# Attention output products by column halves, and the layout of three PSUM banks

## The chip, the cores and the metric

The kernel runs on one core of one Trainium2 chip. The metric is the time of one execution on the device in microseconds (us). Runs are compared by their medians; the profile is of one execution.

## The reference

One transformer block with adaptive layer norm: sliding-window attention over a key/value cache, then a gated feed-forward part. x is 2048 x 576, 32 query heads share 16 key/value heads of width 128, the window is the last 512 keys, and the feed-forward width is 4608.

```python
mod = (_silu(c) @ w_mod).reshape(c.shape[0], 6, 1, -1)
sa, ca, ga, sb, cb, gb = (mod[:, 0], mod[:, 1], mod[:, 2], mod[:, 3], mod[:, 4], mod[:, 5])
h = _layernorm(x, axis=-1) * (1 + ca) + sa
x = x + ga * _A_ref(h, A_k_cache, A_v_cache, A_wq, A_wo)
h = _layernorm(x, axis=-1) * (1 + cb) + sb
x = x + gb * _B_ref(h, B_w1, B_w3, B_w2)
...
# _A_ref: q = x @ wq by heads; softmax(q k^T * Dh**-0.5) v; heads side by side @ wo
# _B_ref: (silu(x @ w1) * (x @ w3)) @ w2
```

## The kernel before

The 2048 rows are four blocks of 512 (b), each of four row tiles of 128 (t). Every product is done in float16 pieces, a high and a low part, so one product is three matmuls: high x high, high x low, low x high.

**Slots and steps.** A slot is one query head on one row block: 128 slots, two heads of a group one after the other, and such two slots are a pair. The main loop runs over slots i and, in each, over four steps t = 0 to 3. The instructions of every engine stand in the order in which this loop writes them; nothing is reordered later. In step t of slot i TensorE (PE) gets: at t = 1 the transposes of one tile of the slot before (`turn`, into a PSUM tile named `pt`); three matmuls for the scores of row tile t (`pss`); at t = 0 to 2 a third of the next slot's query projection (`pq`); one piece of an older pair's output product; then the step's tasks. At the slot's end come twelve matmuls of the value product (`values`, `po`).

**The output product.** `attend_out` multiplies the two normalized heads `o` of a pair (slots 2*pair and 2*pair + 1) with `wo` (128 x 576 for each head) and adds the result to `acc`. A row tile takes two steps, one head in each (j = 0, then j = 1): `back` goes through the three float16 combinations and, in each, through the two column halves of 288. The halves lie in the two PSUM banks of the tile `E` (its name in the trace is `pe`). After j = 1, VectorE (DVE) adds both halves to `acc` with one SCALAR_TENSOR_TENSOR (L617), called the add below. The products of a pair start at step t = 2 of slot 2*pair + 4, so j = 0 falls on even t and j = 1 on odd t. Some steps also put a small matmul for a scale factor into a corner of E (`sum_peaks`, `in_total`, `out_total`), which DVE copies out right after the add.

**PSUM.** Eight banks: two tiles `A` (`pq`, `po`, `py`), two tiles `S` (`pss`, `px`), the two-bank tile E, and two one-bank tiles `T` (`pt`). The T tiles serve `turn` and also the transposes of normalized rows, five per row block (m = 0 to 4; `turn_rows`, L257), from which ScalarE (ACT), and in the kernel's first microseconds DVE too, makes h: `modulate` (L272 later, L266 to L270 at the start), `modulate_first` (L284 and L286, for the very first block) and `store_h` (L656). For blocks 2 and 3, and again for blocks 0 and 1 before the feed-forward part, these five stand in the steps t = 0, 1, 2 of one slot and t = 0, 1 of the next, after the step's output product. When attention ends, the T tiles make room for a second two-bank tile for the feed-forward part (`turning.close()`).

**Waits.** The tile layer that records the program puts semaphore waits before an instruction, for every tile that it reads or writes: what another engine still does with that tile has to be done first.

Of the kernel before, what the change touches and what calls it, by code (L numbers as in the profile page):

```python
# [20 lines left out]
P = 128  # L21
# [27 lines left out]
def tile_block(  # L49
# [110 lines left out]
    def mod_cols(wm, name, one, tag):  # L160

        ps = t_bank() if tag == "T" else bank(tag, f"ps_{name}")
# [12 lines left out]
    def mod_rows(wm, kind):  # L175

        vec = gate_rows[kind]
        wm = wm[0]
        for h in range(2):
            for d in (0, 3):  # L180
                nc.tensor.matmul(
                    E[:, h, :HALF], ones, wm[:, d, h * HALF : (h + 1) * HALF], start=d == 0, stop=d == 3
                )
        nc.vector.tensor_copy(half_split(vec), E[:, :, :HALF])
        return vec
# [67 lines left out]
    def turn_rows(b, m, tag):  # L253

        ps = t_bank() if tag == "T" else bank(tag, "ps_n")
        for t in range(ST):
            nc.tensor.transpose(ps[:, t * P : (t + 1) * P], norms[b][1][t][:, m * P : (m + 1) * P], ident)  # L257
        return ps
# [69 lines left out]
    def sum_peaks(g, lo, hi, ps=None):  # L328

        ps = E[:, 1, 400:416] if ps is None else ps  # L330
        nc.tensor.matmul(ps[:, lo:hi], peak_ones, tops[g][:, lo:hi], start=True, stop=True)

    def take_sums(g, lo, hi, ps=None):

        ps = E[:, 1, 400:416] if ps is None else ps
        nc.vector.tensor_copy(peaks[g][:, 5 + lo : 5 + hi], ps[:, lo:hi])
# [116 lines left out]
    def back(ps, o, w, t, first, last):  # L453

        rows = slice(t * P, (t + 1) * P)
        for n, (x, y) in enumerate(((0, 0), (0, 1), (1, 0))):
            for h in range(2):
                nc.tensor.matmul(  # L458
                    ps[:, h, :HALF],
                    o[:, x, rows],  # L460
                    w[:, y, h * HALF : (h + 1) * HALF],
                    start=first and n == 0,
                    stop=last and n == 2,
                )
# [144 lines left out]
    def attend_out(pair, t, j, total):  # L609
        u, _, b = slots[2 * pair]  # L610
        lane[0] += j == 0
        ps = spare()
        back(ps, state[2 * pair + j]["o"], wos[u][:, j], t, j == 0, j == 1)
        if j == 1:
            run(*total)
            a = half_split(acc[b][:, t, :])
            nc.vector.scalar_tensor_tensor(  # L617
                a, ps[:, :, :HALF], factors[:, uses[u][0], 2:3], a, op0=ALU.mult, op1=ALU.add
            )
# [3 lines left out]
    for pair in range(n // 2):  # L623
        for k in range(2 * ST):
# [6 lines left out]
            outs.setdefault(when, []).append((pair, *divmod(k, 2)))  # L631
# [17 lines left out]
    def store_h(b, m, tag, tag_out):  # L649
# [9 lines left out]
        store_later(hd[b][m * P : m * P + n, :], hf[:n], ("s", b, m) if tag == "T" else None)  # L659
# [485 lines left out]
    lane = [0, ()]  # L1145

# [12 lines left out]
    def in_total(f):  # L1159

        m = peak_cols[:, 4 * (f % 2) :][:, :4]
        for part in range(2):
            peak = m[:, 2 * part + 1 : 2 * part + 2]
            nc.tensor.matmul(
                spare()[:, 1, 408:410], peak.to_broadcast([P, P]), m[:, 2 * part : 2 * part + 2],
# [3 lines left out]
    def in_taken(f):  # L1169
        nc.vector.tensor_copy(stats[:, f, :], spare()[:, 1, 408:410])  # L1170
# [24 lines left out]
    def out_total(p):  # L1195
        nc.tensor.matmul(spare()[:, 1, 410:411], peak_ones, peak_cols[:, 8 + p % 2 : 9 + p % 2], start=True, stop=True)

    def out_taken(p):
        nc.vector.tensor_copy(out_down[:, p : p + 1], spare()[:, 1, 410:411])
# [236 lines left out]
    def make_h(b, m, early=False):  # L1436
        modulate(hT[b], m, turn_rows(b, m, "T"), vecs["shift", "a"], vecs["gain", "a"], early)
# [34 lines left out]
    for b, i in ((0, 111), (1, 114)):  # L1472
        norm(i, b)
        for m in range(DC + 1):
            at(i + 1 + m // 3, m % 3, store_h, b, m, "T", "raw")
# [50 lines left out]
    at(106, 2, make_cols, "shift", "b", 3, 0.0, "T")  # L1526
    at(109, 2, make_cols, "gain", "b", 4, 1.0, "T")
    at(109, 3, lambda: spread_peaks("b", mlp_small))
    at(110, 1, lambda: scale_cols("b", t_bank(), mlp_small, 2.0**-8))
# [24 lines left out]
    turned = [turn_rows(0, m, "TTAAS"[m]) for m in range(DC + 1)]  # L1554
# [44 lines left out]
    for i in range(n + 2):  # L1599
        run(i, -1)  # L1600
        for t in range(ST):
# [121 lines left out]
```

## Time and profile before

| | us |
|---|---|
| median of 3 runs | 2752.52 |
| lowest, highest | 2752.24, 2756.41 |
| the profiled execution's own time | 2752.42 |
| its span | 2750.3 |
| PE busy in it | 2682.3 (98%) |
| DVE busy | 1995.2 (73%) |
| POOL (GpSimd) busy | 1873.1 (68%) |
| ACT busy | 1622.9 (59%) |

In a row of the timeline stand the start in us from the span's start, how long the row's instructions took together, the engine, the line, the operation, out<-in, the shapes, the count, and in brackets the engine's idle time before it and what ended that. A matmul's end is modelled and overlaps the next one's start, so an idle time in brackets is smaller than the pause from start to start.

### The profile page before, as it was taken

Reading aid. Unit: us, or ns where it says so; the run is one execution under the profiler, and the core shown is the slowest. Engines: PE = TensorE matmul, PEld = TensorE weight load, DVE = VectorE, ACT = ScalarE, POOL = GpSimd, SP = SyncE. Lnnn points to the kernel's source line nnn. Section 1 sums busy time; section 2 is a strip of 40 time slices with the busy share of each in tenths; the row PEclk is TensorE's granted clock in tenths of the full one; section 3 lists DMA queues with packets and bytes.
Section 4 is the critical chain, followed back from the end, with each engine's and each line's share of the span. In section 5 each row is a group of like instructions: output and inputs, shape, how many; then the busy total and the mean of one; then the engine's idle time right before and its main releaser. Section 6 shows DMA issues by size and latency. Waiting matters only on the chain.

```text
span 2750.3 us, 44762 instructions
## 1 busy us (share of the span) xinstructions
PE 2682.3 (98%) x15406; PEld 1511.8 (55%) x15406; DVE 1995.2 (73%) x3550; ACT 1622.9 (59%) x3026; POOL 1873.1 (68%) x1745
## 2 busy tenths in 40 slices
PE   6899999999999999999999999999999999999998
PEld 3455555555555555555555555555555555555555
DVE  7877787878787787887876667777776666566566
ACT  6776778777777778777677635544443323333332
POOL 4677888888888877777669637688774465334435
PEclk9999999999999999999999999999999999999999
DMA  6778888778787888978879945656643434333332
GB/s 196 174 171 198 195 180 192 168 182 188 171 187 165 190 193 193 214 178 208 194 182 219 241 134 171 200 165 201 208 160 107 157 122 129 102 103 111 105 109 85
DMA packets 593460, 463.84 MB, mean 169 GB/s; under 512 B 442704, under 2 KB 472528, under 8 KB 592208
## 3 DMA queue, kind: packets, MB, share of 16 engines
q1 hardware_dynamic: 592944, 460.69, 65.4%
q8 instruction: 121, 1.98, 0.3%
q14 instruction: 107, 0.88, 0.1%
q10 hardware_dynamic: 288, 0.30, 0.0%
HBM read 264.19 MB, written 95.99 MB: 131 GB/s over the span
## 4 chain that ended last, share of the span: by engine, by line
PE 50%; DVE 2%; POOL 2%; issue 1%; DMA 1%; ACT 1%; SPq 0%; POOLq 0%; DVEq 0%; ACTq 0%
PE py L874 15%; PE px L874 11%; PE pf L959 6%; PE pe L959 6%; PE pe L458 3%; PE po L587 3%; PE pss L508 2%; PE pq L435 2%; DMA r<-row 1%; PE pt L548 0%; POOL acc L913 0%; PE pq L439 0%; DMA row<-l 0%; DVE table L512 0%; POOL sums L913 0%
## 5 line engine op out<-in xcount | busy, mean ns | idle before, releaser
L562 POOL TENSOR_TENSOR hp<-p,hp 128x512 f16<-128x512 f32 x384 | 448.8, 1171 | 269.6 <-ACT hp L557 154.1
L525 ACT ACTIVATE p<-pss,table,factors 128x512 f32<-128x512 f32 x512 | 396.8, 775 | 355.1 <-DVE table L513 175.7
L874 PEld LDWEIGHTS <-wset 128*128 128x128 f16 x3528 | 344.2, 98 | 337.4 <-issue 4.0
L512 DVE TENSOR_REDUCE table<-pss 128x1 f32<-128x512 f32 x512 | 350.3, 684 | 199.4 <-PE pss L508 198.8
L874 PE MATMUL py<-hset,wset 128*128 128x512 f16 x2016 | 482.1, 379 | 0.0
L458 PE MATMUL pe<-o 128*128 128x288 f16 x3024 | 453.4, 286 | 11.6 <-DVE acc L617 10.7
L508 PE MATMUL pss<-k,qT 128*128 128x512 f16 x1536 | 418.0, 380 | 13.2 <-ACT p L525 10.6
L458 PEld LDWEIGHTS <-o 128*128 128x128 f16 x3072 | 300.8, 98 | 186.1 <-issue 17.5
L587 PE MATMUL po<-ptw,v 128*128 128x512 f16 x1536 | 358.6, 381 | 7.8 <-DVE ptw L577 2.7
L874 PE MATMUL px<-hset,wset 128*128 128x512 f16 x1512 | 361.5, 379 | 2.1 <-ACT p L525 2.1
L94 POOL TENSOR_TENSOR akv<-u,akv 128x512 f16<-128x512 f32 x141 | 164.8, 1178 | 178.4 <-ACT akv L93 170.5
L435 PE MATMUL pq<-hT,wq 128*128 128x512 f16 x1092 | 280.6, 379 | 0.0
L557 ACT CAST hp<-p 128x512 f16<-128x512 f32 x384 | 237.3, 618 | 14.1 <-DMA ptw<-hp 0.9
L587 PEld LDWEIGHTS <-v 128*128 128x128 f16 x1536 | 147.8, 98 | 175.0 <-issue 16.2
L959 PEld LDWEIGHTS <-akv 128*128 128x128 f16 x1728 | 169.1, 98 | 89.3 <-issue 0.8
L508 PEld LDWEIGHTS <-qT 128*128 128x128 f16 x1536 | 147.6, 98 | 127.2 <-issue 14.8
L617 DVE SCALAR_TENSOR_TENSOR acc<-pe,factors,acc 128x576 f32<-128x576 f32 x252 | 204.3, 811 | 4.8 <-PE pe L458 4.8
L607 POOL TENSOR_TENSOR o<-on,o 128x512 f16<-128x512 f32 x128 | 150.2, 1174 | 54.0 <-ACT o L606 52.0
L435 PEld LDWEIGHTS <-wq 128*128 128x128 f16 x1092 | 106.9, 98 | 127.4 <-issue 1.0
L953 DVE SCALAR_TENSOR_TENSOR acc<-pf,table,acc 128x576 f32<-128x576 f32 x140 | 113.5, 811 | 79.3 <-PE pf L959 79.3
L1052 ACT COPY u<-py 128x512 f32<-128x512 f32 x72 | 42.2, 586 | 201.3 <-PE py L874 199.4
L1045 ACT ACTIVATE s<-s,table 128x512 f32<-128x512 f32 x72 | 52.0, 722 | 175.1 <-DVE s L1044 175.0
(254 smaller groups left out, 4789.0 us busy)
## 6 DMA issues: line engine op xcount, KB each, us to landing
wset<-wd SPq DMA_DIRECT2D x213, 320.0 KB, 3.2
r<-row SPq DMA_DIRECT2D x128, 256.0 KB, 3.9
oset<-od SPq DMA_DIRECT2D x106, 288.0 KB, 3.2
wraw<-in_w SPq DMA_DIRECT2D x36, 768.0 KB, 5.5
wd<-wmade SPq DMA_DIRECT2D x75, 320.0 KB, 3.2
wset<-wd SPq DMA_DIRECT2D x71, 160.0 KB, 2.2
w2raw<-in_w SPq DMA_DIRECT2D x19, 576.0 KB, 5.2
wd<-ring SPq DMA_DIRECT2D x33, 320.0 KB, 2.8
```

The lines of the kernel that those rows point to most:

```text
L94: eng.tensor_sub(halves[:, 1], src, halves[:, 0])
L435: nc.tensor.matmul(ps, w[:, k // 2, m, :], hT[:, DC + m if k == 1 else m, :], start=s == 0, stop=False)
L458: nc.tensor.matmul(ps[:, h, :HALF], o[:, x, rows], w[:, y, h * HALF : (h + 1) * HALF], start=first and n == 0, stop=last and n == 2,)
L508: nc.tensor.matmul(pss, q[:, x, rows], k[:, y, :], start=n == 0, stop=n == 2)
L512: nc.vector.tensor_reduce(nm[:, 0:1], pss, axis=AX.X, op=ALU.max, negate=True)
L525: nc.scalar.activation(p, pss, AF.Exp, bias=nm[:, 1:2], scale=factor, accum_out=st["l"][:, t : t + 1])
L557: nc.scalar.copy(hp[:, 0, :], state[i]["p", t])
L562: nc.gpsimd.tensor_sub(hp[:, 1, :], state[i].pop(("p", t)), hp[:, 0, :])
L587: nc.tensor.matmul(po, v[:, x, c, :], pt[:, y, c, :], start=c == 0 and n == 0, stop=c == KC - 1 and n == 2)
L617: nc.vector.scalar_tensor_tensor(a, ps[:, :, :HALF], factors[:, uses[u][0], 2:3], a, op0=ALU.mult, op1=ALU.add)
L874: nc.tensor.matmul(ps, w[:, a, :], h[:, b, :], start=start and n == 0, stop=stop and n == 6, skip_group_check=True)
L959: nc.tensor.matmul(ps[:, h, :HALF], a[:, rows], w[:, b, :], start=m == 0, stop=m == 2)
```

## The change

E becomes a tile of three banks, in the pool that T was in, and T has one buffer instead of two. The output product of a row tile is now cut by column halves: the first step does the right half (h = 1) for both heads, the second the left half (h = 0) for both. The left half lies in bank 0, the right half in bank 1 or 2, in turn from tile to tile (`lane[0]`). The add reads both halves through one strided view, banks 0 and 1 or banks 0 and 2. The transposes of normalized rows, the column sums of the modulation (`mod_cols`) and `scale_cols` now write the bank of E that is not in use for a right half (`idle()`); the very first ones and those of the second block go to banks 1 and 2 by name. The small sums go to bank 0.

```diff
-    E = psum.tile([P, 2, 512], F32, tag="E", name="pe", bufs=1)
     turning = ExitStack()
-    tpool = turning.enter_context(tc.tile_pool(name="tpool", bufs=2, space=PSUM))
-
-    def t_bank():
-        return tpool.tile([P, 512], F32, tag="T", name="pt")
+    tpool = turning.enter_context(tc.tile_pool(name="tpool", bufs=1, space=PSUM))
+    E = tpool.tile([P, 3, 512], F32, tag="E", name="pe")
+    lane = [1, ()]
+
+    def both_halves():
+        return lane[1][lane[0] % 2][:, :, :HALF] if lane[1] else E[:, 0 : lane[0] + 1 : lane[0], :HALF]
+
+    def idle():
+        return E[:, 3 - lane[0], :]
...
     def turn_rows(b, m, tag):
-        ps = t_bank() if tag == "T" else bank(tag, "ps_n")
+        ps = idle() if tag == "E" else E[:, int(tag), :] if tag in "012" else bank(tag, "ps_n")
...
-    def back(ps, o, w, t, first, last):
+    def back(ps, o, w, t, h, first, last):
         rows = slice(t * P, (t + 1) * P)
         for n, (x, y) in enumerate(((0, 0), (0, 1), (1, 0))):
-            for h in range(2):
-                nc.tensor.matmul(
-                    ps[:, h, :HALF],
...
+            nc.tensor.matmul(
+                ps,
...
-        ps = st["t"] = t_bank().rearrange("p (j n) -> p j n", j=KC)
+        ps = st["t"] = tpool.tile([P, KC, P], F32, tag="T", name="pt")
...
-    def attend_out(pair, t, j, total):
+    def attend_out(pair, t, h, total):
         u, _, b = slots[2 * pair]
-        lane[0] += j == 0
-        ps = spare()
-        back(ps, state[2 * pair + j]["o"], wos[u][:, j], t, j == 0, j == 1)
-        if j == 1:
+        if h:
+            lane[0] = 3 - lane[0]
+        for j in range(2):
+            back(both_halves()[:, h], state[2 * pair + j]["o"], wos[u][:, j], t, h, j == 0, j == 1)
+        if not h:
             run(*total)
             a = half_split(acc[b][:, t, :])
             nc.vector.scalar_tensor_tensor(
-                a, ps[:, :, :HALF], factors[:, uses[u][0], 2:3], a, op0=ALU.mult, op1=ALU.add
+                a, both_halves(), factors[:, uses[u][0], 2:3], a, op0=ALU.mult, op1=ALU.add
             )
...
-            outs.setdefault(when, []).append((pair, *divmod(k, 2)))
+            outs.setdefault(when, []).append((pair, k // 2, 1 - k % 2))
...
     def make_h(b, m, early=False):
-        modulate(hT[b], m, turn_rows(b, m, "T"), vecs["shift", "a"], vecs["gain", "a"], early)
+        modulate(hT[b], m, turn_rows(b, m, str(1 + m % 2) if early else "E"), vecs["shift", "a"], vecs["gain", "a"], early)
...
-    at(110, 1, lambda: scale_cols("b", t_bank(), mlp_small, 2.0**-8))
+    at(110, 1, lambda: scale_cols("b", idle(), mlp_small, 2.0**-8))
...
-    turned = [turn_rows(0, m, "TTAAS"[m]) for m in range(DC + 1)]
+    turned = [turn_rows(0, m, "12AAS"[m]) for m in range(DC + 1)]
...
-                    lane[1] = (E, after.tile([P, 2, 512], F32, tag="T2", name="pf"))
+                    lane[1] = tuple(after.tile([P, 2, 512], F32, tag=tag, name=tag) for tag in ("pe", "pf"))
```

Four places in the order of PE's instructions, each before and then after the change. In brackets stand the semaphores that a row waits for. L257 became L262, L458 became L462, L508 became L512, L435 and L445 became L440 and L450.

The start of a row tile's output product, in a plain slot: the end of a third of a query (`pq`), then the first matmuls of the product (`pe<-o`).

```order
L435 MATMUL pq<-hT,wq 128x512
L458 LDWEIGHTS o
L458 MATMUL pe<-o 128x288 [waits DVE_49]
L458 LDWEIGHTS o
L458 MATMUL pe<-o 128x288
```

```order
L440 MATMUL pq<-hT,wq 128x512
L462 LDWEIGHTS o
L462 MATMUL pe<-o 128x288 [waits DVE_49]
L462 LDWEIGHTS o
L462 MATMUL pe<-o 128x288
```

The matmul is now the first of a right half, in a bank that the tile before did not use. It keeps a wait for DVE, and the count that it waits for is, before and after, that of the add of the tile before (or, where a small sum was copied out behind that add, of the copy).

Step t = 1 of the first of the slots with transposes of normalized rows: the end of the output product, the four transposes (`<-ident,xn`), the next scores.

```order
L458 MATMUL pe<-o 128x288
L257 MATMUL pt<-ident,xn 128x128 [waits Activation_49]
L257 MATMUL pt<-ident,xn 128x128 x3
L508 LDWEIGHTS qT
L508 MATMUL pss<-k,qT 128x512
```

```order
L462 MATMUL pe<-o 128x288
L262 MATMUL pe<-ident,xn 128x128 [waits DVE_49]
L262 MATMUL pe<-ident,xn 128x128 x3
L512 LDWEIGHTS qT
L512 MATMUL pss<-k,qT 128x512
```

The wait for an older read of a T tile became a wait for DVE; its count is that of the add whose products stand right ahead of it.

Step t = 2 of the same slot and the start of t = 3: the transposes, the scores, and the second piece of the output product.

```order
L257 MATMUL pt<-ident,xn 128x128 [waits Activation_49]
L257 MATMUL pt<-ident,xn 128x128 x3
L508 LDWEIGHTS qT
L508 MATMUL pss<-k,qT 128x512
L508 LDWEIGHTS qT
L508 MATMUL pss<-k,qT 128x512
L508 LDWEIGHTS qT
L508 MATMUL pss<-k,qT 128x512
L458 LDWEIGHTS o
L458 MATMUL pe<-o 128x288
L458 LDWEIGHTS o
```

```order
L262 MATMUL pe<-ident,xn 128x128 x4
L512 LDWEIGHTS qT
L512 MATMUL pss<-k,qT 128x512
L512 LDWEIGHTS qT
L512 MATMUL pss<-k,qT 128x512
L512 LDWEIGHTS qT
L512 MATMUL pss<-k,qT 128x512
L462 LDWEIGHTS o
L462 MATMUL pe<-o 128x288 [waits Activation_49]
L462 LDWEIGHTS o
```

The second piece, now a left half in bank 0, got a wait for ACT; its count is that of ACT's read (`modulate`) of the transposes four rows up.

The start of the kernel: a warming matmul, then the first query (`pe<-hT,wq`).

```order
L223 MATMUL ps_warm<-ident,ones 128x128 x2
L445 LDWEIGHTS wq [waits Activation_49]
L445 MATMUL pe<-hT,wq 128x512 [waits Activation_49]
L445 LDWEIGHTS wq
L445 MATMUL pe<-hT,wq 128x512 [waits DVE_49]
L445 LDWEIGHTS wq
L445 MATMUL pe<-hT,wq 128x512 [waits Activation_49]
```

```order
L228 MATMUL ps_warm<-ident,ones 128x128 x2
L450 LDWEIGHTS wq [waits Activation_49]
L450 MATMUL pe<-hT,wq 128x512 [waits Activation_49]
L450 LDWEIGHTS wq
L450 MATMUL pe<-hT,wq 128x512
L450 LDWEIGHTS wq
L450 MATMUL pe<-hT,wq 128x512
```

Before, each matmul waits for the piece of h that it reads. Now the first waits for ACT's fifth read in `modulate_first`, the last one that touches a bank of E, and the next ones need no wait of their own.

More of the change, by code (lines that the diff above doesn't have):

```diff
@@ L160, in mod_cols @@
     def mod_cols(wm, name, one, tag):
-        ps = t_bank() if tag == "T" else bank(tag, f"ps_{name}")
+        ps = idle() if tag == "E" else bank(tag, f"ps_{name}")
         wm = wm[0]
@@ L181, in mod_rows @@
                 nc.tensor.matmul(
-                    E[:, h, :HALF], ones, wm[:, d, h * HALF : (h + 1) * HALF], start=d == 0, stop=d == 3
+                    ps[:, h], ones, wm[:, d, h * HALF : (h + 1) * HALF], start=d == 0, stop=d == 3
                 )
-        nc.vector.tensor_copy(half_split(vec), E[:, :, :HALF])
+        nc.vector.tensor_copy(half_split(vec), ps)
         return vec
@@ L451, in project_first @@
                     nc.tensor.matmul(ps, w[:, k, DC, :], hT[:, 2 * DC, :], start=False, stop=False)
-    def back(ps, o, w, t, first, last):
+    def back(ps, o, w, t, h, first, last):
         rows = slice(t * P, (t + 1) * P)
         for n, (x, y) in enumerate(((0, 0), (0, 1), (1, 0))):
-            for h in range(2):
-                nc.tensor.matmul(
-                    ps[:, h, :HALF],
[L460 to L464, printed above, removed]
+            nc.tensor.matmul(
+                ps,
+                o[:, x, rows],
+                w[:, y, h * HALF : (h + 1) * HALF],
+                start=first and n == 0,
+                stop=last and n == 2,
+            )
     QP = (range(0, 5), range(5, 10), range(10, 14))
@@ L1164, in in_total @@
             nc.tensor.matmul(
-                spare()[:, 1, 408:410], peak.to_broadcast([P, P]), m[:, 2 * part : 2 * part + 2],
+                spare()[:, 0, 408:410], peak.to_broadcast([P, P]), m[:, 2 * part : 2 * part + 2],
                 start=part == 0, stop=part == 1,
@@ L1195, in out_total @@
     def out_total(p):
-        nc.tensor.matmul(spare()[:, 1, 410:411], peak_ones, peak_cols[:, 8 + p % 2 : 9 + p % 2], start=True, stop=True)
+        nc.tensor.matmul(spare()[:, 0, 410:411], peak_ones, peak_cols[:, 8 + p % 2 : 9 + p % 2], start=True, stop=True)
     def out_taken(p):
-        nc.vector.tensor_copy(out_down[:, p : p + 1], spare()[:, 1, 410:411])
+        nc.vector.tensor_copy(out_down[:, p : p + 1], spare()[:, 0, 410:411])
     def out_scale(p):
```

16 lines of the change are left out of this document (8 added, 8 removed).

## The prediction

> **What bounds the kernel now.** I read the page's busy shares first, then PE's waits, then the rows of the places that the change touches.
>
> ```profile
> PE 2682.3 (98%) x15406; PEld 1511.8 (55%) x15406; DVE 1995.2 (73%) x3550; ACT 1622.9 (59%) x3026; POOL 1873.1 (68%) x1745
> L458 PE MATMUL pe<-o 128*128 128x288 f16 x3024 | 453.4, 286 | 11.6 <-DVE acc L617 10.7
> PE pe L458 <- DVE acc L617: 10.7, 11, 2.0
> PE pss L508 <- ACT p L525: 10.6, 14, 2.6
> ```
>
> PE is the bound; any time that it gains or loses is the kernel's, unless a later wait takes it back. All that the output product can give back is its wait for the add of the tile before: 10.7 us in 11 places. That is the ceiling of what a free third bank could give.
>
> **The change part by part.**
>
> *The wait for the add stays: 0.* The right half goes to an unused bank, but in the built program its first matmul still waits for the add of the tile before, for nearly all tiles, exactly as the first matmul did. Waits are made for the tile E as a whole, not for its banks. So I take nothing off. Bounds: 0 and -10.7.
>
> *Six matmuls a step, in one bank: 0.* The feed-forward product does three in one bank one after the other:
>
> ```profile
> 2003.24 0.90 PE L959 MATMUL pf<-oset,aah 128*128 128x288 f16 x6
> ```
>
> Six take 0.90 there, as in the attention rows below, where the banks alternate.
>
> *Five transposes per row block now write E.* The first block's rows, PE, then DVE, then ACT:
>
> ```profile
> 141.76 0.90 PE L458 MATMUL pe<-o 128*128 128x288 f16 x6
> 142.49 0.60 PE L257 MATMUL pt<-ident,xn 128*128 128x128 f32 x4
> 142.93 0.81 PE L508 MATMUL pss<-k,qT 128*128 128x512 f16 x3
> 146.26 0.90 PE L458 MATMUL pe<-o 128*128 128x288 f16 x6
> ...
> 142.74 0.82 DVE L617 SCALAR_TENSOR_TENSOR acc<-pe,factors,acc 128x576 f32<-128x576 f32 x1
> 144.45 0.64 DVE L512 TENSOR_REDUCE table<-pss 128x1 f32<-128x512 f32 x1
> ...
> 145.37 0.78 ACT L525 ACTIVATE p<-pss,table,factors 128x512 f32<-128x512 f32 x1 [0.57 <-DVE table L513]
> 147.28 0.77 ACT L272 ACTIVATE hf<-pt,mod_a 128x512 f32<-128x512 f32 x1
> ```
>
> (a) At t = 1 the transposes now wait for the add just issued. They started at 142.49; the add ends at 142.74 + 0.82 = 143.56, so PE stands 1.07. This happens twice per block (m = 1 and m = 4) in four blocks: eight times. The last of the eight:
>
> ```profile
> 1441.99 0.60 PE L257 MATMUL pt<-ident,xn 128*128 128x128 f32 x4
> 1442.24 0.81 DVE L617 SCALAR_TENSOR_TENSOR acc<-pe,factors,acc 128x576 f32<-128x576 f32 x1
> ```
>
> 1442.24 + 0.81 - 1441.99 = 1.06. Eight times 1.07 is 8.6 us. Queued behind the waiting transposes are the next scores, so DVE's maximum and ACT's exponential start later too.
>
> (b) At t = 3 the left half waits for ACT's read of the transposes made at t = 2. In the first block the read ended at 147.28 + 0.77 = 148.05 and the product started at 146.26: 1.79 late. The other three blocks:
>
> ```profile
> 183.61 0.90 PE L458 MATMUL pe<-o 128*128 128x288 f16 x6
> 184.82 0.77 ACT L272 ACTIVATE hf<-pt,mod_a 128x512 f32<-128x512 f32 x1
> ...
> 1394.83 0.90 PE L458 MATMUL pe<-o 128*128 128x288 f16 x6
> 1395.44 0.77 ACT L656 ACTIVATE hf<-pt,shift_b,gain_b 128x512 f32<-128x512 f32 x1
> ...
> 1432.87 0.90 PE L458 MATMUL pe<-o 128*128 128x288 f16 x6
> 1434.31 0.77 ACT L656 ACTIVATE hf<-pt,shift_b,gain_b 128x512 f32<-128x512 f32 x1
> ```
>
> 1.98, 1.38 and 2.21; with the first 7.36 us. This holds PE's delay of (a) at m = 1 inside it, as far as ACT's read does not move. How far it moves: in the first block the scores would end at about 144.7 instead of being long ready when DVE took them at 144.45, so the chain maximum, exponential, read moves by some 0.35; in the others I estimate 0 to 0.6 by the same sum. So (a) at m = 1 and (b) together delay PE by 7.36 + 1.5 = 8.9 us, between 7.4 (the read does not move) and 11.7 (it moves by all of 1.07 each time). With (a) at m = 4, four times 1.07 = 4.3, the blocks cost 13.2 us, from 11.7 to 16.0.
>
> (c) The transposes of t = 0 come 0.73 + 0.65 + 1.08 us of PE work before the next product and are read by then or 0.2 late: 0.
>
> *The first query.* It waited for its first piece of h; now it waits for the last read of E in `modulate_first`, and reads of E by ACT and DVE also go one after the other.
>
> ```profile
> 24.90 3.57 PE L445 MATMUL pe<-hT,wq 128*128 128x512 f16 x8 [1.45 <-ACT hT L286]
> 29.78 0.93 PE L448 MATMUL pe<-hT,wq 128*128 128x512 f16 x3 [0.26 <-POOL hT L295]
> 24.07 0.78 ACT L286 ACTIVATE hT<-pt,mod_a 128x512 f16<-128x512 f32 x1 [1.13 <-DVE mod_a L1122]
> 26.74 0.79 ACT L286 ACTIVATE hf<-pt,mod_a 128x512 f32<-128x512 f32 x1
> 24.07 0.81 DVE L284 TENSOR_SCALAR hT<-pt,mod_a 128x512 f16<-128x512 f32 x1
> 25.52 0.80 DVE L284 TENSOR_SCALAR hf<-pt,mod_a 128x512 f32<-128x512 f32 x1
> ```
>
> DVE's first read starts after ACT's, 0.78 later; its second, at 25.52, then ends at 27.1, and ACT's fifth read goes from there to 27.9. PE starts at 27.95 instead of 24.90: 3.05. The wait of 0.26 for low parts goes, since they are ready by then: 2.8. Bounds: 1.5 (if full clock catches the second half of the query) and 3.1.
>
> *The second block's transposes* (slots 0 and 1) had two T tiles; as one tile E they go one at a time, turn, read, turn.
>
> ```profile
> 39.76 0.63 PE L257 MATMUL pt<-ident,xn 128*128 128x128 f32 x4 [0.96 <-DVE hT L268]
> 43.31 1.11 PE L257 MATMUL pt<-ident,xn 128*128 128x128 f32 x4 [2.92 <-ACT hT L270]
> 46.94 0.60 PE L257 MATMUL pt<-ident,xn 128*128 128x128 f32 x4
> 45.30 0.78 ACT L270 ACTIVATE hT<-pt,mod_a 128x512 f16<-128x512 f32 x1 [1.33 <-DVE hf L266]
> ```
>
> m = 2 moves from 39.76 to the place of m = 3 at 43.31; m = 3 comes after the read at 45.30 + 0.78 = 46.1; m = 4 a round of 2.3 to 2.8 later, at 48.4 to 48.9 instead of 46.94. I take 1.7, from 0.9 to 2.8 (all of 46.1 - 43.31).
>
> *`scale_cols`* writes E at t = 1 and waits for the add in the same way; 1.05, of which a later wait of 0.19 to 0.36 pays back a part: 0.8, from 0 to 1.1.
>
> *The second head is needed a step earlier.* `o` of the second head comes from POOL.
>
> ```profile
> 721.69 1.16 POOL L607 TENSOR_TENSOR o<-on,o 128x512 f16<-128x512 f32 x1
> 721.47 0.90 PE L458 MATMUL pe<-o 128*128 128x288 f16 x6
> 724.49 1.68 PE L587 MATMUL po<-ptw,v 128*128 128x512 f16 x7 [0.74 <-DMA ptw<-hp]
> ```
>
> Of 62 pairs, three have it late for the new place, this one by 0.9 (needed about 721.96, ready 722.85). Here the next wait, 0.74 at 724.49, takes most of it. 0.5 in all, from 0 to 2.5.
>
> *One T buffer: 0.* A slot's turn now waits for the slot before to be done with T, a whole slot (some 12 us) ago.
>
> Sum: 13.2 + 2.8 + 1.7 + 0.8 + 0.5 = 19.0 us. The profiled execution took 2752.42, 0.1 below the median; with the change 2771.4.
>
> **The clock.** A pause can cost more than itself:
>
> ```profile
> 578.60 1.53 PE L458 MATMUL pe<-o 128*128 128x288 f16 x6 [1.98 <-DVE acc L617]
> 576.00:578.60 2.60, 0.62 (x4) 0.20 (x2) 1.84 (x3) 0.70 (x2) 2.60 (x3) 1.00 1.05 270
> 578.70:582.10 3.40, 3.40 (x13) 1.81 (x12) 3.36 (x6) 1.13 (x3) 0.94 (x2) 0.50 1.01 196
> ```
>
> After 1.98 us of idle PE the granted clock was 0.50 for 3.4 us, which costs 1.7. The new pauses are 1.1 to 2 us long; I count none of these drops and keep two, 3.4 us, for the upper end. The Trainium skill (TensorE: Matmul & The Clock Gate, "What's actually happening") says that the clock halves after an idle window of about 3.4 us; by that rule none of the new pauses would halve it. The trace shows a shorter pause that did, so the measurement decides, and the upper end keeps its 3.4.
>
> **The rivals.** *Banks are guarded singly (faster).* If the right half's first matmul did not wait, up to 10.7 us would be there. Part is given back at the slot's end: at 578.60 the value product waits for DVE anyway.
>
> ```profile
> 580.76 0.68 DVE L577 TENSOR_TENSOR ptw<-pt,ptw 128x512 f16<-128x512 f32 x1
> 582.44 2.75 PE L587 MATMUL po<-ptw,v 128*128 128x512 f16 x12
> ```
>
> Its third matmul needs this subtraction's end, 581.44; having two matmuls done by then it gains about 1.4 of the 2.1 us from start to start. By that ratio 10.7 becomes 7, and the new waits vanish as well: 2752.4 - 7 = 2745. It decides at one wait, that of the right half's first matmul, and the program has it. Chance 0.03. The Trainium skill (PSUM — Partial Sum Buffer, "PSUM bank collisions raise a hardware error") gives the rule to guard PSUM by bank and quadrant; by it neither this wait nor those of the transposes would be needed. No trace here shows whether the chip needs them; the program has them either way.
>
> *Paid back (no change).* The new pauses let DVE, ACT and POOL get ahead, and later waits of PE shrink by as much. PE has such waits (10.7 and 10.6 above), but between 143 and 195 and between 1442 and 1490 hardly any; 2753 to 2757. Chance 0.05.
>
> *Only the waits for DVE count.* If ACT's reads come early because PE's pauses free them, (b) vanishes: 8.6 + 2.8 + 1.7 + 0.8 = 13.9, so 2766. Chance 0.2; the reads stand behind the exponential of the same step, which speaks against it.
>
> *Clock drops after most pauses.* Four at 1.7 on top: 2778. Chance 0.1.
>
> **How the numbers follow.** The forecast with all terms has 0.6, and the rivals 0.03, 0.05, 0.2, 0.1; 0.02 is for faster by something unseen. Low end of the terms: 11.7 + 1.5 + 0.9 = 14.1, or 9.5 without (b): 2762. High end: 16.0 + 3.1 + 2.8 + 1.1 + 2.5 + 3.4 = 28.9: 2781. The range 2761 to 2781 leaves out the first two rivals and little more. A measurement tells 0.2%, 5.5 us, from no change: faster 0.05, same 0.05, slower 0.90. I predict 2771.
>
> **What would show it.** In the changed kernel's trace: PE's waits keep the output product's wait for the add, near 10 us (right) or lose it (wrong); the transposes wait for the add, eight times about 1.1 us; the left half waits for ACT's read four times, 1 to 2 us; the first query starts near 28 us instead of 24.90, and the first scores come about 2.8 us later. I would be wrong if PE's idle time at these places is there but the span is not longer, or if ACT's reads move ahead of the exponential.

## The result, and the profile after

| | before | after |
|---|---|---|
| median, us (5 runs each) | 2754.33 | 2772.47 |
| lowest, highest | 2752.24, 2756.41 | 2771.22, 2777.55 |
| ratio to before, 95% interval | | 1.0066, 1.0054 to 1.0077 |
| profiled execution: its time, span | 2752.42, 2750.3 | 2771.22, 2769.2 |

The change costs 0.66%, 18 us; 2771 was forecast, 19.0 more than before. Two lines of the page after (busy shares; the output product's group), then PE's waits (us in total, times, longest): the one that answers to before's, and the larger ones that are new or come from another place.

```profile
PE 2681.5 (97%) x15406; PEld 1510.1 (55%) x15406; DVE 1993.4 (72%) x3550; ACT 1624.3 (59%) x3026; POOL 1875.3 (68%) x1745
L462 PE MATMUL pe<-o 128*128 128x288 f16 x3024 | 452.6, 286 | 19.1 <-DVE acc L622 9.2
```

```profile
PE pe L462 <- DVE acc L622: 9.2, 10, 2.0
PE pe L262 <- DVE acc L622: 6.0, 6, 1.1
PE pe L262 <- DVE table L1173: 1.1, 1, 1.1
PE pe L262 <- DVE us L341: 1.1, 1, 1.1
PE pe L450 <- ACT hf L291: 5.0, 1, 5.0
PE pe L462 <- ACT hf L661: 3.0, 2, 1.9
PE pe L462 <- ACT hf L277: 2.0, 3, 1.1
PE pe L462 <- POOL o L611: 2.8, 3, 1.1
```

PE does the same work (2681.5 against 2682.3 us). The wait for the add, all that a third bank could have given back, is still 9.2 us (10.7 before). Below it stand waits that before has not: the transposes for the add, eight times about 1.1 us (six for the add itself and two for a small copy right behind it); the first query for the last read of E (1.4 for an earlier read before); the left half for ACT's reads of h; and three times the second head, which comes late from POOL. The wait of the second block's transposes for ACT's read, not shown here, grows from 2.9 to 4.8 us.

The same places as in the prediction, timeline after. First block: step t = 1 with its transposes, then the left half at t = 3.

```profile
146.11 0.90 PE L462 MATMUL pe<-o 128*128 128x288 f16 x6
147.11 0.82 DVE L622 SCALAR_TENSOR_TENSOR acc<-pe,factors,acc 128x576 f32<-128x576 f32 x1
147.99 0.65 PE L262 MATMUL pe<-ident,xn 128*128 128x128 f32 x4 [0.98 <-DVE acc L622]
148.48 0.81 PE L512 MATMUL pss<-k,qT 128*128 128x512 f16 x3
...
152.22 0.77 ACT L277 ACTIVATE hf<-pe,mod_a 128x512 f32<-128x512 f32 x1
153.04 0.90 PE L462 MATMUL pe<-o 128*128 128x288 f16 x6 [1.07 <-ACT hf L277]
```

The transposes follow the product by 147.99 - 146.11 = 1.88 us; before it was 142.49 - 141.76 = 0.73. They start when the add ends (147.11 + 0.82 = 147.93). The scores come 5.55 us later than before's at 142.93, the product ahead of them 4.35 later: 1.20 lost in this one step. At t = 3 the left half starts when ACT's read ends (152.99) and stands 153.04 - 146.26 = 6.78 late: 1.23 more.

The start: first query, its scores, the second block's transposes, and the next slot's scores.

```profile
27.81 3.34 PE L450 MATMUL pe<-hT,wq 128*128 128x512 f16 x8 [5.02 <-ACT hf L291]
33.13 1.12 PE L512 MATMUL pss<-k,qT 128*128 128x512 f16 x3 [0.69 <-ACT qT L496]
45.05 1.11 PE L262 MATMUL pe<-ident,xn 128*128 128x128 f32 x4 [2.98 <-ACT hT L275]
47.98 1.11 PE L262 MATMUL pe<-ident,xn 128*128 128x128 f32 x4 [1.82 <-ACT hT L275]
48.89 1.49 PE L512 MATMUL pss<-k,qT 128*128 128x512 f16 x3
```

The same two scores before:

```profile
31.39 1.12 PE L508 MATMUL pss<-k,qT 128*128 128x512 f16 x3 [0.69 <-ACT qT L492]
44.21 1.49 PE L508 MATMUL pss<-k,qT 128*128 128x512 f16 x3
```

They are 1.74 and 4.68 us late. Carried on for all 512 steps in the same way (start of a step's scores after, less before), the shift grows and falls by these amounts:

| place | forecast, us | shift of PE, us |
|---|---|---|
| first query | 2.8 | 1.7 |
| second block's transposes | 1.7 | 2.9 |
| eight times the transposes at t = 1 | 8.6 | 9.8 (1.20 to 1.27 each) |
| four times the left half at t = 3 | 4.6 | 5.4 (1.23, 0.90, 1.23, 2.05) |
| scale_cols | 0.8 | 0.8 (1.19, of which 0.35 comes back) |
| second head a step earlier, and all else | 0.5 | -1.8 |
| sum | 19.0 | 18.8 |

(4.6 is the forecast's 8.9 for (a) at m = 1 and (b) together less 4.3 for the former.) The spans differ by 18.9. The last row but one holds one rise that was not forecast: at the end of slot 12, two steps behind the last transposes, the value product waits 1.24 us for a DMA, which costs 1.10.

### The profile page after: what moved, and what is told of

It is laid out like the page before. It is cut to its first block, busy times and chain, and to the rows that moved or that the text cites. A ratio compares the mean times of both kernels' runs of the same rounds, so it can differ in the third digit from the quotient of the medians.

```text
span 2769.2 us, 44886 instructions
## 1 busy us (share of the span) xinstructions
PE 2681.5 (97%) x15406; PEld 1510.1 (55%) x15406; DVE 1993.4 (72%) x3550; ACT 1624.3 (59%) x3026; POOL 1875.3 (68%) x1745
## 3 DMA queue, kind: packets, MB, share of 16 engines
q8 instruction: 121, 1.98, 0.3%
## 4 chain that ended last, share of the span: by engine, by line
PE 51%; DVE 3%; ACT 1%; issue 1%; POOL 1%; DMA 0%; SPq 0%; DVEq 0%; POOLq 0%; ACTq 0%
PE py L879 15%; PE px L879 11%; PE pe L964 7%; PE pf L964 6%; PE pe L462 3%; PE po L591 3%; PE pss L512 2%; PE pq L440 2%; DVE table L516 0%; PE pt L552 0%; DVE on L600 0%; PE pq L444 0%; DVE acc L622 0%; DMA r<-row 0%; DVE acc L975 0%
## 5 line engine op out<-in xcount | busy, mean ns | idle before, releaser
L462 PE MATMUL pe<-o 128*128 128x288 f16 x3024 | 452.6, 286 | 19.1 <-DVE acc L622 9.2
L512 PE MATMUL pss<-k,qT 128*128 128x512 f16 x1536 | 417.3, 379 | 13.2 <-ACT p L529 10.6
L462 PEld LDWEIGHTS <-o 128*128 128x128 f16 x3072 | 300.3, 98 | 193.5 <-issue 23.6
L440 PE MATMUL pq<-hT,wq 128*128 128x512 f16 x1092 | 280.8, 380 | 0.0
L512 PEld LDWEIGHTS <-qT 128*128 128x128 f16 x1536 | 147.4, 98 | 126.7 <-issue 15.1
L440 PEld LDWEIGHTS <-wq 128*128 128x128 f16 x1092 | 107.0, 98 | 127.6 <-issue 1.3
L958 DVE SCALAR_TENSOR_TENSOR acc<-pe,table,acc 128x576 f32<-128x576 f32 x140 | 113.5, 810 | 79.2 <-PE pe L964 79.2
```

The lines of the kernel that those rows point to most:

```text
L440: nc.tensor.matmul(ps, w[:, k // 2, m, :], hT[:, DC + m if k == 1 else m, :], start=s == 0, stop=False)
L462: nc.tensor.matmul(ps, o[:, x, rows], w[:, y, h * HALF : (h + 1) * HALF], start=first and n == 0, stop=last and n == 2,)
L512: nc.tensor.matmul(pss, q[:, x, rows], k[:, y, :], start=n == 0, stop=n == 2)
```

## Experiments

All were compared in five rounds with the kernel before on the same chip; its median was 2753.1 to 2753.8.

### The order alone

```diff
 # before, E with two banks, T with two buffers
...
-        lane[0] += j == 0
+        lane[0] += h
         ps = spare()
-        back(ps, state[2 * pair + j]["o"], wos[u][:, j], t, j == 0, j == 1)
-        if j == 1:
+        for j in range(2):
+            back(ps[:, h, :HALF], state[2 * pair + j]["o"], wos[u][:, j], t, h, j == 0, j == 1)
+        if not h:
...
-            outs.setdefault(when, []).append((pair, *divmod(k, 2)))
+            outs.setdefault(when, []).append((pair, k // 2, 1 - k % 2))
```

> The kernel before with the column-half order alone: the first step of a row tile does the right half for both heads, the second the left half; E keeps two banks and T two buffers, the transposes stay in T. Theory (the added 19 us are waits that treat the three-bank tile as one): the order itself costs only the second head that is needed a step earlier, so the time is that of before plus 0 to 2 us (ratio 1.000 to 1.001), PE's wait of the output product for the add stays near 10.7 us in 11 places, and no transposes wait for the add. Rival (six matmuls in a row into one bank, or the order, cost time): 0.08 us for each of 248 steps or more, 15 to 20 us, ratio 1.005 to 1.007.

Measured: 2754.42, ratio 0.9998 (0.9989 to 1.0007). PE's wait there, a little below the expected 10.7 us in 11 places:

```profile
PE pe L457 <- DVE acc L617: 8.7, 9, 2.0
```

The order costs nothing that can be measured, six matmuls in one bank included. The three late second heads are in the trace (2.2 us of waits; shifts of 1.24, 0.84 and 0.66), and behind each the shift falls again, by 0.65, 0.47 and 1.74.

### The layout alone

```diff
 # before, products by heads as they were
-    E = psum.tile([P, 2, 512], F32, tag="E", name="pe", bufs=1)
...
-    tpool = turning.enter_context(tc.tile_pool(name="tpool", bufs=2, space=PSUM))
+    tpool = turning.enter_context(tc.tile_pool(name="tpool", bufs=1, space=PSUM))
+    E = tpool.tile([P, 3, 512], F32, tag="E", name="pe")
     def t_bank():
-        return tpool.tile([P, 512], F32, tag="T", name="pt")
+        return E[:, 2, :]
...
-    turned = [turn_rows(0, m, "TTAAS"[m]) for m in range(DC + 1)]
+    turned = [turn_rows(0, m, "12AAS"[m]) for m in range(DC + 1)]
...
```

The small sums go to bank 0, as in the changed kernel. The add reads banks 0 and 1, and the transposes of the main loop write bank 2.

> The kernel before with the layout alone: E a tile of three banks, output products by heads as before in banks 0 and 1, the transposes of normalized rows in bank 2, the first ones and the second block's in banks 1 and 2, one T buffer. Theory (waits for the whole tile): nearly all of the loss, 1.7 (first query) + 2.9 (second block) + 15 (transposes that wait for the add, products that wait for ACT's read) = 17 to 20 us, ratio 1.006 to 1.007, with PE's wait of the transposes for the add near 6 us in 8 places. Rival (the layout does no harm by itself, only together with the order): 0 to 3 us, ratio 1.000 to 1.001.

Measured: 2773.68, ratio 1.0080 (1.0067 to 1.0092), a little over the 17 to 20 us expected.

```profile
PE pe L458 <- DVE acc L617: 10.0, 10, 2.6
PE pe L257 <- DVE acc L617: 6.0, 6, 1.1
PE pe L445 <- ACT hf L286: 5.0, 1, 5.0
PE pe L458 <- ACT hf L656: 3.0, 2, 1.9
PE pe L458 <- ACT hf L272: 2.0, 3, 1.1
```

The whole loss comes with the layout, with the same waits as in the changed kernel, the last four rows to the tenth. Transposes that write bank 2 wait for an add that reads only banks 0 and 1, so it is not an overlap of what they touch that makes the wait, but the one tile.

### The same banks in tiles of their own

```diff
 # the order alone, and:
-    tpool = turning.enter_context(tc.tile_pool(name="tpool", bufs=2, space=PSUM))
+    tpool = turning.enter_context(tc.tile_pool(name="tpool", bufs=1, space=PSUM))
-    def t_bank():
-        return tpool.tile([P, 512], F32, tag="T", name="pt")
+    def t_bank(tag="H"):
+        return tpool.tile([P, 512], F32, tag=tag, name="pt" if tag == "T" else "ph")
...
-        ps = t_bank() if tag == "T" else bank(tag, "ps_n")
+        ps = t_bank("HT"[m % 2] if m < 4 and b < 2 and not hd else "H") if tag == "T" else bank(tag, "ps_n")
...
-        ps = st["t"] = t_bank().rearrange("p (j n) -> p j n", j=KC)
+        ps = st["t"] = t_bank("T").rearrange("p (j n) -> p j n", j=KC)
```

> The column-half order with the same eight banks as the changed kernel, but in tiles of their own: two banks for E, one for the transposes of normalized rows, one T buffer. Nothing alternates. Theory (the loss is the sharing of one tile, not the one T buffer or the single bank for transposes): the time of before plus 0 to 2 us, ratio 1.000 to 1.001, and no transposes that wait for the add. Rival (one buffer for the turns, or one bank for the transposes, costs): 5 us or more, ratio over 1.002.

Measured: 2753.07, ratio 0.9997 (0.9988 to 1.0006). One T buffer costs nothing, and neither does a single bank for the transposes in the main loop (at the start they alternate between it and T). No row of PE's waits there has transposes that wait for the add. What costs is that the bank belongs to the tile that the add reads.

### The start mended

```diff
 # the changed kernel, and:
+        if tag == "T":
+            ps = tpool.tile([P, 512], F32, tag="T", name="pt")
...
-            st["q"] = bank("A", "pq") if i else E[:, 0, :]
+            st["q"] = bank("A", "pq") if i else tpool.tile([P, 512], F32, tag="T", name="pe")
...
-    modulate(hT[b], m, turn_rows(b, m, str(1 + m % 2) if early else "E"), vecs["shift", "a"], vecs["gain", "a"], early)
+    modulate(hT[b], m, turn_rows(b, m, "1T2T1"[m] if early else "E"), vecs["shift", "a"], vecs["gain", "a"], early)
```

> The changed kernel with its start alone mended: the first query goes to the T tile, and the second block's transposes alternate between E and T. Theory: the two waits of the start, 1.74 and 2.93 us in the shift of PE, go, and nothing later takes them back: 4.0 to 4.7 us below the changed kernel, ratio to the kernel before 1.0048 to 1.0052. Rival (the start's loss is hidden by a later wait anyway, and its place is taken by other pauses): within 1.5 us of the changed kernel, ratio 1.006 to 1.007.

Measured: 2769.15, ratio 1.0055 (1.0040 to 1.0069), 3.3 us under the changed kernel's median; the intervals overlap, so the time alone does not decide. The trace does for the two places:

```profile
PE pe L453 <- ACT hT L294: 1.2, 1, 1.2
44.44 1.48 PE L515 MATMUL pss<-k,qT 128*128 128x512 f16 x3
```

The first query waits 1.2 instead of 5.0 us, and the second slot's scores come at 44.44 instead of 48.89, 4.45 earlier (44.21 before). Of that, PE keeps 3.0 at slot 2 and 1.9 at the end of the spans: later pauses took more than half back. My figure of 4.0 to 4.7 was too high.

### Three tiles of one bank

```diff
 # the changed kernel, and:
-    E = tpool.tile([P, 3, 512], F32, tag="E", name="pe")
+    E = [tpool.tile([P, 512], F32, tag=f"E{k}", name=f"pe{k}") for k in range(3)]
...
-            a = half_split(acc[b][:, t, :])
-            nc.vector.scalar_tensor_tensor(
-                a, both_halves(), factors[:, uses[u][0], 2:3], a, op0=ALU.mult, op1=ALU.add
-            )
+            for side in (1, 0):
+                a = half_split(acc[b][:, t, :])[:, side]
+                nc.vector.scalar_tensor_tensor(
+                    a, both_halves()[side][:, :HALF], factors[:, uses[u][0], 2:3], a, op0=ALU.mult, op1=ALU.add
+                )
```

> The changed kernel with three tiles of one bank each instead of one tile of three banks, so that each bank is guarded for itself; the add becomes two, one for each half of 288 columns, at the same place. Theory: all the waits for the whole tile go, the loss of 19 us with them, and the right half no longer waits for the add (10.7 us in 11 places before, of which I expect 7 to come through); the second add costs DVE some 0.3 us for each of 248 tiles, off the path. Time of before minus 3 to minus 8 us, ratio 0.997 to 0.999. Rival A (the wait for the add is repaid at the next wait): ratio 0.9995 to 1.001. Rival B (the added DVE time reaches PE by the maximum and the exponential of the scores): 3 to 20 us slower than before, ratio 1.001 to 1.007.

Measured: 2766.48, ratio 1.0042 (1.0029 to 1.0054): the theory failed, rival B came true. The waits for the whole tile are gone and the wait for the add is down, but two others have grown (10.6 and 2.7 before):

```profile
PE pss L514 <- ACT p L531: 14.5, 20, 1.9
PE po L593 <- DVE ptw L583: 9.9, 20, 1.0
PE pe L464 <- DVE acc L625: 3.9, 3, 2.2
L625 DVE SCALAR_TENSOR_TENSOR acc<-pe,factors,acc 128x288 f32<-128x288 f32 x504 | 236.1, 511 | 5.1 <-PE pe L464 5.1
```

Each add is 0.511 long, but the second starts before the first has ended: for 252 tiles the two keep DVE busy 236.1 us, where one add kept it 204.3 before, 0.13 more a tile. Two smaller waits, 3.5 us in four places, are for ACT's reads of the transposes: there the next right half goes into the very bank that holds them. What was open: did the freed banks give something that the adds took, or nothing?

### Two adds without free banks

```diff
 # the order alone (E with two banks, one tile), and:
-            nc.vector.scalar_tensor_tensor(
-                a, ps[:, :, :HALF], factors[:, uses[u][0], 2:3], a, op0=ALU.mult, op1=ALU.add
-            )
+            for side in (1, 0):
+                nc.vector.scalar_tensor_tensor(
+                    a[:, side], ps[:, side, :HALF], factors[:, uses[u][0], 2:3], a[:, side], op0=ALU.mult, op1=ALU.add
+                )
```

> The kernel before with the column-half order and two banks, as in the run of the order alone, and the add cut in two of 288 columns each, 0.51 us apiece, 1.02 in place of 0.82. It is the control for the three tiles of one bank, which took 2766.5: the same DVE work, but the banks not freed. Theory (a free bank gives nothing, since PE then waits for DVE at the value product; the loss of the three tiles is DVE's longer adds): the same as the three tiles within 3 us, 2763 to 2770, ratio 1.0035 to 1.006. Rival A (the free bank gives 7 us and the adds cost 20): 2771 to 2778, ratio 1.0065 to 1.009. Rival B (the adds cost nothing, the three tiles lose elsewhere): under 2757, ratio under 1.001.

Measured: 2765.76, ratio 1.0044 (1.0031 to 1.0056), the same as the three tiles. So the second add costs 12.6 us by itself, since the order alone cost nothing, and the free banks gave nothing that shows. The two intervals leave room for about 5 us either way, and the 3.5 us of waits for ACT's reads, which only the three tiles have, may hide as much of a gain. A large stall shows where a free bank's gain goes. First this kernel, then the three tiles, the same slot:

```profile
969.49 1.06 DVE L595 TENSOR_TENSOR on<-po,r 128x512 f32<-128x512 f32 x1 [2.60 <-POOL o L606]
971.45 0.90 PE L457 MATMUL pe<-o 128*128 128x288 f16 x6 [2.22 <-DVE acc L618]
973.62 3.05 PE L586 MATMUL po<-ptw,v 128*128 128x512 f16 x12
976.51 0.81 PE L507 MATMUL pss<-k,qT 128*128 128x512 f16 x3
```

```profile
967.25 1.08 DVE L602 TENSOR_TENSOR on<-po,r 128x512 f32<-128x512 f32 x1 [2.60 <-POOL o L613]
969.24 0.90 PE L464 MATMUL pe<-o 128*128 128x288 f16 x6 [0.85 <-DVE acc L625]
970.70 0.18 PE L1170 MATMUL pe<-peak_cols 128*128 128x2 bf16 x1 [0.56 <-DVE peak_cols L1161]
972.13 2.32 PE L593 MATMUL po<-ptw,v 128*128 128x512 f16 x10 [0.75 <-DVE ptw L583]
974.29 0.81 PE L514 MATMUL pss<-k,qT 128*128 128x512 f16 x3
```

In both, DVE stands 2.60 us in its multiply `on`, which waits for GpSimd, and everything behind it in DVE's order is late. With one tile PE takes that as one wait of 2.22 for the add. With free banks it goes on and meets three others, 0.85 + 0.56 + 0.75 = 2.16, the last in the value product, which needs DVE's subtraction. From the multiply's start to the next slot's scores it is 7.02 and 7.04 us. In this stall the wait for the add is not a want of a bank, but DVE's lateness, and PE meets it at the next thing that it needs of DVE.

### The right half's add a step earlier

```diff
 # the three tiles of one bank, and:
         if not h:
             run(*total)
-            for side in (1, 0):
...
+        a = half_split(acc[b][:, t, :])[:, h]
+        nc.vector.scalar_tensor_tensor(
+            a, both_halves()[h][:, :HALF], factors[:, uses[u][0], 2:3], a, op0=ALU.mult, op1=ALU.add
+        )
```

> The three tiles of one bank, with the right half's add put right after the right half, one step earlier, so that only 0.51 us of adding stands behind the left half instead of 1.02. Theory (what the three tiles lose is the longer DVE time between the left half and the value product): 2 to 8 us less than the three tiles, 2758 to 2764, ratio 1.0015 to 1.004. Rival (DVE's total sets it, wherever the add stands): 2765 to 2768, ratio 1.004 to 1.005.

Measured: 2760.23, ratio 1.0025 (1.0017 to 1.0033), as expected: nearly half of the added cost goes when less of DVE's work lies between the left half and the value product, although DVE is busy longer than in any other run (2040.8 us). It is still slower than before.

### The blocked multiply moved

If the multiply is what makes DVE late, its place should matter. Two places, in the kernel before:

```diff
-            if 2 <= i <= n and t == 1:
-                normalize(i - 2)
...
 # first version: behind the output product of t = 1
             for piece in outs.get((i, t), ()):
                 attend_out(*piece, (i, ("total", t)))
+            if 2 <= i <= n and t == 1:
+                normalize(i - 2)
 # second version: at t = 2
                 turn_low(i - 1, ST - 1)
+                if i > 1:
+                    normalize(i - 2)
```

> The kernel before, with the normalization of a head (the DVE multiply of po by r, 1.08 us, which in all large pauses stands in front of the late add and waits up to 2.5 us for GpSimd's subtraction of o) moved in step t = 1 from ahead of the output product's add to behind it. Theory (the add was late because this multiply blocks DVE, not for want of a bank; and the subtraction of the low part of the weights at t = 2, which the value product needs, is still behind it): PE's wait for the add falls from 10.7 us to under 4, its wait at the value product rises, and the time is that of before less 0 to 4 us, ratio 0.9985 to 1.000. Rival (the wait for the add is the whole price): 7 to 10 us less, ratio 0.9965 to 0.9975.

> The same multiply moved further, to step t = 2 behind the subtraction that the value product needs. Theory: now neither the add nor the subtraction stands behind the blocked multiply, so both waits of PE go: 5 to 9 us less than before, ratio 0.9967 to 0.998. Rival (the head is normalized too late, so the split of o, the query's low part or the exponentials behind it on ACT and DVE wait instead): ratio 0.9995 to 1.003.

Measured: 2781.04, ratio 1.0102 (1.0088 to 1.0116), and 2798.35, ratio 1.0165 (1.0151 to 1.0179). Both theories and both rivals missed. The first version's waits, PE's and one of DVE's:

```profile
PE po L587 <- DVE ptw L577: 13.0, 22, 1.5
PE pe L458 <- DVE table L1170: 5.7, 14, 0.5
PE pe L458 <- DVE us L336: 5.7, 12, 0.7
DVE acc L617 <- PE pe L458: 74.6, 86, 3.0
```

PE's in the second version:

```profile
PE po L587 <- ACT hp L557: 35.3, 44, 2.0
PE po L587 <- DVE on L596: 28.6, 38, 2.0
```

The wait for the add did go: in both versions no row of PE names it for the output product any more. But the add, now first, waits for PE's product: DVE stands 74.6 us there, before 4.8. In its old place the multiply filled that time; moved, it comes after it and pushes back the small copies that the next product waits for (5.7 + 5.7) and the subtraction (13.0). In the second version the value product also waits for the multiply itself, which must have read the older `po` out of its bank. That is more than the 28.6 us of its own row:

```profile
710.43 1.06 DVE L596 TENSOR_TENSOR on<-po,r 128x512 f32<-128x512 f32 x1
711.55 2.76 PE L587 MATMUL po<-ptw,v 128*128 128x512 f16 x12 [0.91 <-ACT hp L557]
```

The multiply ends at 711.49 and the product starts 0.06 later. It does so in all 38 places of the one row and in 40 of the 44 of the other; ACT's cast `hp` only happens to end nearer. So nearly all of 35.3 + 28.6 us is the wait for the multiply. I had looked at the few slots in which the multiply was blocked, not at the many in which its place was good.

The same move in the changed kernel:

```diff
 # the changed kernel
-            if 2 <= i <= n and t == 1:
-                normalize(i - 2)
...
                 turn_low(i - 1, ST - 1)
+                if i > 1:
+                    normalize(i - 2)
```

> The changed kernel with the multiply in the same new place. Theory: the two edits are independent, so it gains what the kernel before gains and keeps the change's loss: 2763 to 2768, ratio to the kernel before 1.0035 to 1.0055, with the eight waits of the transposes for the add still near 6 us and more. Rival (without the blocked multiply the adds come early and the loss of the layout shrinks to the start's 4.7): 2750 to 2755, ratio 0.999 to 1.001.

Measured: 2821.24, ratio 1.0247 (1.0233 to 1.0261), 22.9 us over the same move in the kernel before. The level missed by as much as the move did; that the change's loss stays beside it, here a few us larger, is what the theory said and the rival denied. The eight waits of the transposes are there, 6.0 us in six places, 1.1 and 1.1, as in the changed kernel.

No version beat the kernel before.

## Why the prediction was right, and where its terms were off

*The wait for the add stays: right.* 9.2 us in 10 places, in the changed kernel. The one place fewer is slot 121: there DVE's multiply waited 2.07 us for a DMA (`r`) before and 0.55 after, and PE's wait of 1.59 for the add behind it is gone. It is not the bank that made the difference, since the layout alone and the order alone lack that wait too. The bound beside it, up to 10.7 to gain, was wrong, and so was the price of the rival of banks guarded singly: its working gave back a part at the value product, 10.7 to 7. The three tiles against the two adds say that nearly all comes back, with the room of some 5 us named there. So with banks guarded singly I would now expect about the time of before, not 2745; with a single add it was not run.

*Six matmuls in one bank, one T buffer: 0, right*, shown by the order alone and by the tiles of their own.

*Transposes in E: right in place and number, too small by 2.0 us* (15.2 against 13.2, inside its bounds of 11.7 to 16.0). A step lost 1.20 to 1.27, not 1.07: in the first, the add ended 1.09 late for the transposes, PE started 0.06 behind it, and they took 0.49 instead of 0.44 to the scores. And ACT's reads moved with PE by more than the estimate. What a block lost at m = 1 and t = 3, less what the read was late before, is 1.20 + 1.23 - 1.79 = 0.64, then 0.12, 1.05 and 1.04: 2.9 us in all, where I had put 1.5. (The reading beside that estimate is off by 0.1: the scores would have ended at 142.93 + 0.81 + 1.07 = 144.8, which gives the 0.35 that was used.)

*First query: 2.8, measured 1.7.* PE's start was right (27.81, forecast 27.95). What was over-priced is the work behind it: from its start to the first scores it took 33.13 - 27.81 = 5.32 us instead of 31.39 - 24.90 = 6.49. Of these 1.17, 0.26 is the wait for low parts, which the forecast had taken off. Most of the rest is the clock: before, it was granted at 0.50 from 24.90 to 29.1, over ten of the fourteen matmuls; after, the stretch of the first eight (27.81 to 31.15) had 0.56 on average and the rest 1.00. The forecast's lower bound of 1.5, the full clock in the second half of the query, was the better value.

*Second block: 1.7, measured 2.9, just over its upper bound of 2.8.* The step that failed is the choice of the path's end: I took m = 4, a round later, where the next slot's scores stand right behind m = 3. That one had been put at 46.1 and is at 47.98; 1.74 of the difference is the first query's.

*scale_cols: right. Second head: 0.5*, in the traces 2.8 us of waits in the changed kernel and 2.2 with the order alone, of which a good part is paid back within a slot (1.27 and 0.65, 1.26 and 0.91 at the first two places); the order alone bounds it at 0.07% of the time, 1.9 us.

*The clock.* In the main loop none of the new pauses halved it, as the sum had it. At the second block's transposes it stayed at 0.50 for 6.8 us (44.43 to 51.26) instead of 3.4 (42.81 to 46.22 before), which cost little: one step of scores later the shift is 4.85 instead of 4.68. What I had not counted is that the drop at 578.60 might not come again; it did not, and at slots 44 and 45 the shift falls by 1.4 us (the last section says why). With the 1.5 at slot 121 that is 2.9 us. The order alone, compared with the same trace of before, falls by 1.4 and 1.7 at the same places, so these 2.9 us come from that one traced execution of before, not from the change.

So the total was met to 1.5 us by terms that were off by 1 to 2 us in both directions, and by falls that were in no term. The mechanism and the places were right; that the sum came so close is in part luck. That the added time comes from the sharing of one tile is shown, by the layout alone and the tiles of their own. How the 15.2 us divide between the transposes' waits and those of the left half is read from the traces and was not tried apart.

## What to carry over

Put into one tile only what may wait for each other: where waits are made by tile, a bank that is free on the chip is not free in the program, and each use by another engine becomes a stop. Before buying a buffer for a wait, ask what the late engine is late with and what the waiting engine needs of it next; if a slow chain on that engine feeds both, the wait only moves. And an instruction that blocks an engine in a few rounds may be filling a gap in all the others: count the time that it would wait behind its neighbour before moving it.

## What the runs showed of the hardware

In these traces a drop of the granted clock goes not with the length of a pause of PE, but with how long PE worked in a fixed step of time. Before, 1.98 us of idle at 578.60 were followed by 3.4 us at 0.50. The same stall after the change, 1.99 us up to 591.70, and the one of 2.22 us up to 971.45 with two adds were not. In each of the twelve traces the granted clock changes only at points that lie whole multiples of 3.41 us apart. In the step before the drop PE was busy for 1.43 us (the granted clock is the third number from the end):

```profile
575.29:578.70 3.41, 1.43 (x8) 0.59 (x6) 1.94 (x3) 1.41 (x3) 3.41 (x4) 1.00 0.92 220
```

The two other pauses lie across the border of two steps. After the change:

```profile
587.15:590.56 3.41, 2.56 (x15) 1.30 (x14) 0.91 (x2) 2.30 (x5) 3.41 (x4) 1.00 1.14 256
590.56:593.97 3.41, 2.27 (x18) 1.61 (x18) 3.38 (x7) 0.00 (x0) 2.18 (x3) 1.00 0.95 208
```

With two adds:

```profile
967.52:970.93 3.41, 1.72 (x9) 0.70 (x8) 1.44 (x3) 1.43 (x4) 3.41 (x4) 1.00 1.16 187
970.94:974.34 3.40, 2.76 (x19) 1.70 (x19) 3.37 (x8) 0.55 (x1) 1.43 (x2) 1.00 1.13 209
```

From 100 us on this parts all steps of the twelve traces: each of the 18 drops follows a step in which PE was busy for at most 0.426 of it, and none of the 9360 other steps at full clock, the lowest of them at 0.429, is followed by one. In the first 100 us the two overlap: drops follow steps of up to 0.53, and full clock follows one of 0.42. PE's busy time is in part modelled, and what the chip itself counts is not shown. The Trainium skill (TensorE: Matmul & The Clock Gate, "What's actually happening") says that an idle window of about 3.4 us is needed. The steps have that length, but one in which PE was busy for 0.42 of it was enough for the drop at 578.60, and here the measurement decides.

In the three tiles, transposes into one bank ran beside the add's reads of the two others:

```profile
144.11 0.60 PE L264 MATMUL pe<-ident,xn 128*128 128x128 f32 x4
144.35 0.95 DVE L625 SCALAR_TENSOR_TENSOR acc<-pe,factors,acc 128x288 f32<-128x288 f32 x2
```

That is what the Trainium skill (PSUM — Partial Sum Buffer, "PSUM bank collisions raise a hardware error") allows, a guard by bank and quadrant; the wait for the whole tile in the changed kernel is the program's, not the chip's.

DVE time can be dear although DVE is idle for a quarter of the span, and where it stands counts for more than its amount: with two adds side by side, 35 us more of it (2030.5 against 1995.2) cost 12.6 us; with one of the two a step earlier, 46 us more cost 7.1.
